# Another fixed list of steps for linear attention followed by a Fourier mix and two layers

## The chip, the core and the metric

The kernel runs on one core of one Trainium2 chip. The metric is the time of one execution on the device in microseconds (us); a run gives one such time, and the median of the runs is what is compared. A core has a matmul engine (PE, with its weight loads shown apart as PEld), a vector engine (DVE), a scalar engine (ACT), GpSimd (POOL) and a queue that mostly issues transfers (SP). Each takes its instructions strictly in the order in which they were written into its program, and they wait for one another through semaphores.

## What is computed

There are four batches with eight heads each, a sequence of 768 and a head width of 48. The first half is a linear attention with a decaying state, the second half mixes its output `x` of 768 x 384 by a Fourier transform over both axes, normalises, and adds two layers. The reference, cut to what matters:

```python
f = 1.0 / (1.0 + np.exp(-f_logit))
for t in range(S):
    state = f[:, :, t, :, None] * state + np.einsum('bhd,bhe->bhde', k[:, :, t], v[:, :, t])
    y[:, :, t] = np.einsum('bhd,bhde->bhe', q[:, :, t], state)
...
X = np.fft.fft(np.fft.fft(x, axis=1), axis=2)
u = x + np.real(X)
un = (u - mu) / np.sqrt(var + 1e-06)
out = u + np.maximum(un @ w_ch1, 0.0) @ w_ch2
```

`w_ch1` is 384 x 1536, `w_ch2` 1536 x 384. Both arrive as 64-bit floating-point words and are converted on the chip.

## The kernel before

**The list.** All the work is written as generators that do one step at a time. A string `ORDER` (lines 27 to 48) has 720 words; the loop at lines 975 to 1021 reads it word by word and runs the step that the word names, under a manual schedule. So the order of the words is the order of the instructions in the queue of each engine, and nothing is rearranged afterwards. A step writes its instructions to several queues at once, transfers on SP among them.

**Attention.** A number in the list is the next step of that unit. There are 16 units, one for two heads of one batch, four to a batch. Its steps in turn: (1) exp and ln on ACT (L372, L373); (2) the running sum of the decays on DVE (L379), and its values at the ends of chunks (L380); (3) two exp on ACT (L383, L384) and `te` (L387); (4) q and k scaled on DVE (L391, L392); (5) the scores `sc` on PE (L400); (6) masking on DVE (`copy_predicated`, L404, `at`); (7) products of masked scores with `v` on PE (L559), more scores (L576) and a copy on ACT (L579); (8) more products (L559), and the chunk states `ds` (L599); (9) their running sum on DVE (L607, `stt`); (10) the products of states and q on PE (L616) and five copies on ACT (L625 to L629); (11) transposes on PE (L636) and copies into `x` (L640, L641); (12) and, for two units of each batch, (13) the folding of `x` on DVE (L663 to L669, then L678 to L687), whose results `se`, `xs`, `ce` and `xc` are the inputs of the Fourier transform. `Kn` transposes the keys of unit n (L538, L540), `Ln` with letters loads its f, q, k (L212, L213) or v (L206, L207) on SP.

**Fourier and layers.** `Fn` is the next step of the front of batch n: four products `z` (L724) with copies on ACT, then `mid` (L758) and `mix` (L743) with sums and moments on DVE. `Hn` is the next step of what follows it: moments, normalising on DVE (`un`, L779), transposes on PE (`pt`, L782) and copies (L783). `Pn` is the next step of the two layers: for batch 0 products `up` (L871), and for its first pair of row blocks `po` (L880); for the others a scheme with fewer products that adds blocks first: `ub` (L840), with sums of inputs on DVE (L814), and sums of its results in `h` (L849) or copies (L847). The second layer is `fx` and `fz` (L894), each group followed by sums on DVE (L901 to L947) and by stores (L692, L698, L916, L931).

**Weights.** There are 24 blocks of weights. `r` issues the load of the next raw block into one of three buffers `raw` (L310), `R` three of them; `C` converts a block on ACT (L281), DVE (L283, L284) and POOL (L285). Both `fx` and `fz` need the differences of blocks that `W` makes on DVE (L358 to L361), and `ub` needs those that the words `B` make (L814, in 128 x 512). `V` and `c` read the weights once more, late, and reduce them (L344) for a check of ranges.

**The rest.** `D` is eight matmuls of a constant with itself into an unused part of a bank (L192), the spare products. `I` and `Z` set constants on POOL, `i` loads an identity, `T` and `S` load and sort the tables of the transform (S on POOL). `M` reduces the ranges met into one flag (L962 to L972, with a matmul `turned`, L969). After the list every engine loads the flag (L1023) and branches (L1025) over a rarely needed second computation.

The spare products and the loop of the list, as far as they matter:

```python
def busy():
    for _ in range(8):
        nc.tensor.matmul(spare, lhsT=bound[:, :C], rhs=bound[:, :C], start=not started, stop=True,
...
for word in ORDER.split():
...
    elif kind == "P":
        next(rest[n], None)
```

Of the kernel before, what the change touches and what calls it, by code (L numbers as in the profile page):

```python
# [12 lines left out]
C = 128  # L13
# [11 lines left out]


ORDER = (
# [20 lines left out]
)  # L48


# [1063 lines left out]
```

## Time and profile before

| | us |
|---|---|
| median of three runs | 526.31 |
| lowest and highest run | 525.15, 529.97 |
| the profiled execution, and its span | 526.26 |

In the profile a line is named by its number (L404), a product or buffer by the program's name without its number. "out<-in" gives what is written and read. Waits name the engine and the line that waited and, behind the arrow, what released it; "issue" is time in which an engine waited for nothing that the profile shows. On the timeline a row is its start, its duration, the engine, the line, the operation, the names, the shape and the number of instructions in it, and in brackets the idle time of the engine just ahead.

The execution has three stretches: the front up to the first `z` of batch 0 at 59.5 us, then the rest of batch 0 with all the weights, and from 143 us on the other three batches.

### The profile page before, as it was taken

To read this page: it belongs to the slowest core of one execution; us is meant where nothing else is said; L and a number is where in the kernel's file an instruction comes from. 1 tells how busy PE (TensorE), PEld (TensorE's weight loads), DVE (VectorE), ACT (ScalarE), POOL (GpSimd) and SP (SyncE) were. 2 spreads that over 40 slices of the span, in tenths; PEclk is the share of its full clock that TensorE was granted. 3 is DMA by queue.
4 is the path that set the end of the run, shared out by engine and by line. 5 is a ranking of instruction groups with operands and counts; after the bars stand their busy time and mean duration, and the time that the engine had idled before them with its cause. 6 is when DMAs were issued, how large, how long until landed. Compare 5 with 4: busy or idle time off the path is not lost.

```text
span 526.3 us, 13807 instructions
## 1 busy us (share of the span) xinstructions
PE 494.9 (94%) x5854; PEld 453.4 (86%) x5854; DVE 378.3 (72%) x746; ACT 218.4 (42%) x520; POOL 58.8 (11%) x85
## 2 busy tenths in 40 slices
PE   5878599999999999999999999999999999999994
PEld 4757388866899889999999999999999999999994
DVE  3598989989955368688588776779776667465571
ACT  5567368656331542453435523550431404031220
POOL 3045033551001000000001000000001000010100
PEclk9789699999999999999999999999999999999998
DMA  8957837575010230103212012120610312220200
GB/s 222 268 147 206 210 109 214 161 221 158 6 55 30 68 97 17 54 21 114 77 55 84 1 55 72 46 63 23 206 43 15 107 47 81 83 91 8 84 11 27
DMA packets 20650, 48.15 MB, mean 91 GB/s; under 512 B 3426, under 2 KB 6179, under 8 KB 20579
## 3 DMA queue, kind: packets, MB, share of 16 engines
q1 hardware_dynamic: 19474, 43.63, 29.5%
q0 software_dynamic: 1104, 3.54, 1.8%
q8 instruction: 48, 0.79, 0.6%
q14 instruction: 24, 0.19, 0.1%
HBM read 42.44 MB, written 4.72 MB: 90 GB/s over the span
## 4 chain that ended last, share of the span: by engine, by line
PE 87%; DVE 6%; issue 2%; ACT 2%; DMA 1%; POOL 0%; SPq 0%; DVEq 0%; ACTq 0%
PE ub L840 23%; PE fx L894 16%; PE fz L894 11%; PE up L871 9%; PE z L724 5%; PE y L559 4%; PE mix L743 3%; PE y L616 2%; PE sc L400 2%; PE ds L599 2%; PE po L880 2%; PE yt L636 2%; PE pt L782 1%; PE st L538 1%; PE y L192 1%
## 5 line engine op out<-in xcount | busy, mean ns | idle before, releaser
L849 DVE TENSOR_TENSOR h<-h,ub 128x512 f32<-128x512 f32 x81 | 55.2, 687 | 33.5 <-PE ub L840 24.5
L692 POOL DMA_INDIRECT out_dram<-x,place x16 | 16.4, 1024 | 357.6 <-DVE x L944 224.3
L847 ACT ACTIVATE h<-ub 128x512 f32<-128x512 f32 x54 | 31.9, 591 | 42.3 <-PE ub L840 42.3
L871 PE MATMUL up<-unT,w 128*128 128x256 f32 x216 | 49.4, 382 | 0.0
L840 PE MATMUL ub<-wide,w 128*128 128x128 f32 x360 | 45.0, 276 | 2.3 <-DVE wide L814 2.3
L894 PE MATMUL fx<-block,h 128*128 128x192 f32 x264 | 46.9, 328 | 0.0
L894 PE MATMUL fx<-w,h 128*128 128x192 f32 x264 | 45.5, 327 | 0.0
L840 PEld LDWEIGHTS ub<-wide,w 128*128 128x128 f32 x360 | 42.4, 192 | 3.4 <-PE pt L782 1.3
L871 PEld LDWEIGHTS up<-unT,w 128*128 128x128 f32 x216 | 40.1, 190 | 5.9 <-ACT h L873 0.4
L851 ACT ACTIVATE h<-h 128x512 f32<-128x512 f32 x45 | 28.4, 631 | 38.1 <-DVE h L849 37.7
L894 PEld LDWEIGHTS fx<-block,h 128*128 128x128 f32 x264 | 43.2, 190 | 0.5 <-DVE x L911 0.2
L894 PEld LDWEIGHTS fx<-w,h 128*128 128x128 f32 x264 | 42.7, 190 | 0.4 <-issue 0.2
L285 POOL TENSOR_TENSOR w<-w,raw 128x384 uint32<-128x384 uint32 x24 | 29.4, 1228 | 72.3 <-DVE w L284 39.1
L840 PE MATMUL ub<-unT,w 128*128 128x128 f32 x288 | 37.0, 275 | 0.0
L840 PEld LDWEIGHTS ub<-unT,w 128*128 128x128 f32 x288 | 34.6, 192 | 0.0
L783 ACT COPY unT<-pt 128x384 f32<-128x384 f32 x24 | 11.4, 484 | 46.8 <-PE pt L782 46.6
L840 PE MATMUL ub<-unT,wide 128*128 128x128 f32 x216 | 29.1, 278 | 0.0
L840 PE MATMUL ub<-wide 128*128 128x128 f32 x216 | 28.6, 275 | 0.1
L873 ACT ACTIVATE h<-up 128x256 f32<-128x256 f32 x36 | 13.9, 385 | 33.6 <-PE up L871 22.0
L840 PEld LDWEIGHTS ub<-unT,wide 128*128 128x128 f32 x216 | 26.4, 192 | 0.5
L840 PEld LDWEIGHTS ub<-wide 128*128 128x128 f32 x216 | 26.3, 192 | 0.3 <-PE ub L840 0.3
L379 DVE TENSOR_TENSOR_SCAN W<-g,bound 112x768 f32<-112x768 f32 x12 | 21.0, 1747 | 6.7 <-ACT g L373 6.7
(194 smaller groups left out, 1000.1 us busy)
## 6 DMA issues: line engine op xcount, KB each, us to landing
raw<-in_w_ch_dram SPq DMA_DIRECT2D x24, 384.0 KB, 5.1
v<-in_v_dram SPq DMA_DIRECT2D x16, 288.0 KB
k<-in_w_ch_dram SPq DMA_DIRECT2D x12, 384.0 KB, 3.4
g<-in_w_ch_dram SPq DMA_DIRECT2D x12, 384.0 KB, 3.3
k<-in_qkf_dram SPq DMA_DIRECT2D x14, 288.0 KB
g<-in_qkf_dram SPq DMA_DIRECT2D x12, 288.0 KB, 3.5
q<-in_qkf_dram SPq DMA_DIRECT2D x12, 288.0 KB, 3.3
wide<-in_qkf_dram SPq DMA_DIRECT2D x10, 288.0 KB, 4.7
```

Source lines behind the costliest of these rows:

```text
L285: nc.gpsimd.tensor_tensor(bits, bits, lo, ALU.add)
L379: nc.vector.tensor_tensor_scan(W, g, bound[:R], 0.0, ALU.add, ALU.min)
L559: nc.tensor.matmul(y[FILL[g], c // 3, c % 3 * C + t.start:c % 3 * C + t.stop], lhsT=vals[rows, o:o + (64 if g == 0 else D)], rhs=weights, ...
L692: nc.gpsimd.indirect_dma_start(out=out.rearrange("b s d -> (b s) d"), out_offset=bass.IndirectOffsetOnAxis(ap=place[:, b, i:i + 1], axis=0 ...
L724: nc.tensor.matmul(z[:, cols], lhsT=src[:, j, lo:hi], rhs=tab[:, t, T % 2, cols], start=(i == 0), stop=(i == len(parts) - 1), skip_group_c ...
L743: nc.tensor.matmul(mix[:, o], lhsT=zz[:rows_of[T], T, PLACES[c]], rhs=cd[:rows_of[T], T, :NQ - odd], start=(i == 0), stop=(i == 1))
L840: nc.tensor.matmul(chains[chain][:, m * 128:(m + 1) * 128], lhsT=block(w)[:, m * 128:(m + 1) * 128], rhs=tokens(a), start=(new and m == 0) ...
L847: nc.scalar.activation(out, got, kind, scale=1.0 if how == "=+" else -1.0)
L849: nc.vector.tensor_tensor(out, out, got, ALU.add if how == "+" else ALU.subtract)
L851: nc.scalar.activation(out, out, AF.Relu)
L871: nc.tensor.matmul(pp[:, :256], lhsT=w1[:, kt, m * 128:(m + 1) * 128], rhs=unT[:, kt], start=(kt == 0), stop=(kt == 2))
L894: nc.tensor.matmul(out, lhsT=h[:, m], rhs=blocks[i][:, m], start=(start and m == 0), stop=(m == H - 1), skip_group_check=True)
```

## The change

Only the string `ORDER` differs. It holds the same words, each as many times as before, in another sequence, so every engine gets the same work in another order (and a few instructions that only wait come out otherwise). The diff, cut to the three places that matter here, the start, the way to the first `F0`, and the end:

```diff
-    "L0f Z I 0 L0q L2q D D L1f L0k D 0 D 0 i D 1 L2f 2 0 D D D L0v 0 L1k K0 D 0 0 D L1q 0 1 D r 1 L3fk D "
-    "D D L1v 2 0 L2k 1 D r r D 1 2 1 3 3 0 C K1 1 2 0 C 1 L3q 2 1 3 C L2v 2 r K2 L4fk 3 L3v L5fk 1 2 1 D "
-    "T 2 0 4 3 D C S 1 2 5 3 D 2 3 2 4 K3 3 D L5qv L4qv 5 4 3 2 3 L6fk 3 2 3 5 R 3 F0 F0 4 6 F0 L6qv F0 C "
...
-    "V P3 P3 c P3 V P3 c P3 c P3 P3 V c c P3 P3 P3 P3 P3 P3 M P3 P3 P3 P3 P3 P3 P3 P3"
+    "I L0f 0 0 i L1f 1 0 L0k L0q Z L2f 2 L0v 0 0 L1q 1 1 D L1k 0 K0 0 2 1 L3fk L2q 3 L1v D D 0 L2k 0 2 1 "
+    "1 r 0 L3q K1 L2v D 1 3 2 0 C 1 1 2 2 3 1 D D r 1 L5fk L4fk L3v T 3 2 r K2 L4qv 5 C L6fk 1 3 2 3 4 D "
+    "D 2 5 2 D 3 0 2 K3 4 3 3 D 3 D 2 2 D 3 D 3 L5qv 4 3 5 4 D D D r D D D 5 L7fk S F0 F0 F0 F0 4 C 4 C 6 "
+    "K4 F0 R D D 4 5 7 4 C H0 H0 4 4 5 K5 L6qv H0 C 5 C r 6 r P0 P0 r 5 C 7 6 6 C P0 P0 5 P0 6 C r 6 7 C "
...
+    "P3 P3 P3 P3 P3 P3 P3 P3 P3 P3 P3 P3 P3 P3 P3 P3 P3 P3 P3 P3 P3 P3 P3 V P3 P3 c P3 P3 M"
```

Three places in the queues follow, first as they stood and then as they stand. In a row stands the line, the operation, the names with the numbers of their buffers and the shape.

The vector engine near the start, where units 0 and 1 (`at_91` and `at_92`) are under way; before:

```order
L404 COPY_PREDICATED at_91<-causal,sc_0_237 128x768
L379 SCALAR_TENSOR_TENSOR W_352<-g_86,bound 112x768
L380 TENSOR_TENSOR deep<-g_86,W_352 112x6
L379 SCALAR_TENSOR_TENSOR W_400<-wide,bound 112x768
L380 TENSOR_TENSOR deep<-wide,W_400 112x6
L607 SCALAR_TENSOR_TENSOR stt_403<-ds_341,te_98 112x288
L391 TENSOR_TENSOR q_90<-q_90,g_86 112x768
L392 TENSOR_TENSOR g_86<-W_352,k_88 112x768
L404 COPY_PREDICATED at_92<-causal,sc_0_429 128x768
```

And now:

```order
L379 SCALAR_TENSOR_TENSOR W_198<-g_86,bound 112x768
L380 TENSOR_TENSOR deep<-g_86,W_198 112x6
L404 COPY_PREDICATED at_91<-causal,sc_0_171 128x768
L379 SCALAR_TENSOR_TENSOR W_249<-wide,bound 112x768
L380 TENSOR_TENSOR deep<-wide,W_249 112x6
L391 TENSOR_TENSOR q_90<-q_90,g_86 112x768
L392 TENSOR_TENSOR g_86<-W_198,k_88 112x768
L607 SCALAR_TENSOR_TENSOR stt_319<-ds_306,te_98 112x288
L404 COPY_PREDICATED at_92<-causal,sc_0_324 128x768
```

The scan of unit 1 (`W` of `g_86`) now stands ahead of unit 0's masking, and unit 1's two scalings ahead of the running sum of unit 0's states (L607).

The matmul engine at unit 1's scores (`sc_0_429` before, `sc_0_324` after); before, the last of 48 spare products ahead of them and what follows:

```order
L192 LDWEIGHTS bound
L192 MATMUL y<-bound 128x128
L400 MATMUL sc_0_429<-q_90,g_86 64x64 x24
L616 MATMUL y<-q_89,stt_403 48x128 x10
L538 MATMUL st_483<-ident,g_86 128x112 x5
```

And now:

```order
L599 MATMUL ds_306<-v_165,kT_221 64x48x2
L599 MATMUL ds_306<-v_165,kT_221 48x48x2
L400 MATMUL sc_0_324<-q_90,g_86 64x64 x24
L616 MATMUL y<-q_89,stt_319 48x128 x10
L538 MATMUL st_370<-ident,g_86 128x112 x5
L192 LDWEIGHTS bound
L192 MATMUL y<-bound 128x128
```

The scores of unit 1 now follow unit 0's states at once, and the spare products come behind the transposed keys.

The vector engine at the end of the list; before, with eight steps of `P3` still to come:

```order
L849 TENSOR_TENSOR h_3_2_5090<-h_3_2_5090,ub_2_1_5092 128x4x128
L962 TENSOR_REDUCE part<-deep 112x1
L963 TENSOR_REDUCE part<-hot 112x1
L964 TENSOR_REDUCE most<-small 128x1
L965 TENSOR_SCALAR most<-most 128x1
L966 SCALAR_TENSOR_TENSOR most<-part,most 112x1
L967 SCALAR_TENSOR_TENSOR most<-part,most 112x1
L970 TENSOR_REDUCE most<-turned 1x1
L972 TENSOR_SCALAR flag<-most 1x1
L901 TENSOR_TENSOR s_3_2_5214<-h_3_2_5090 128x768
```

And now:

```order
L344 TENSOR_REDUCE small<-g_85 128x1
L927 TENSOR_TENSOR x_3907<-fx_2_5192,x_3907 128x384
L930 TENSOR_TENSOR x_3907<-fz_2_5210,x_3907 128x192
L962 TENSOR_REDUCE part<-deep 112x1
L963 TENSOR_REDUCE part<-hot 112x1
L964 TENSOR_REDUCE most<-small 128x1
L965 TENSOR_SCALAR most<-most 128x1
L966 SCALAR_TENSOR_TENSOR most<-part,most 112x1
L967 SCALAR_TENSOR_TENSOR most<-part,most 112x1
L970 TENSOR_REDUCE most<-turned 1x1
L972 TENSOR_SCALAR flag<-most 1x1
L1023 TENSOR_LOAD flag
```

The flag is now made behind the last sum of the second layer, and the load of the flag follows it.

32 rows, old and new, of the table ORDER are left out of this document.

## The prediction, made before the changed kernel ran

> **What bounds the kernel now.** I read the page first, then windows by stage, then the waits of DVE and PE at the front, then their timelines. The profiled execution lasted 526.26 us, 0.05 us off the median of the three runs, so the sum needs no correction.
>
> The windows view gives busy time by engine, the granted clock (PEclk) and the DMA share for a stretch:
>
> ```profile
> core 0: us, PE busy (x) PEld busy (x) DVE busy (x) ACT busy (x) POOL busy (x), PEclk, DMA share, GB/s
> 0.00:59.50 59.50, 39.77 (x940) 34.57 (x940) 41.90 (x69) 36.78 (x77) 18.15 (x49) 0.85 0.84 220
> 17.70:24.50 6.80, 6.17 (x69) 5.83 (x70) 2.57 (x3) 3.68 (x6) 0.00 (x0) 0.50 1.04 284
> 55.20:65.50 10.30, 5.96 (x14) 3.89 (x15) 9.65 (x23) 3.77 (x12) 0.00 (x0) 0.50 0.75 205
> 59.50:143.30 83.80, 82.27 (x1084) 64.58 (x1085) 76.48 (x128) 50.46 (x128) 25.73 (x21) 0.96 0.52 146
> 143.30:519.40 376.10, 372.81 (x3832) 354.25 (x3830) 259.55 (x550) 131.18 (x315) 14.87 (x15) 1.00 0.20 60
> ```
>
> From 143.3 to 519.4 us PE is busy in 372.81 of 376.10 us. The edit adds no matmul but moves some, so at most 3.3 us is to be had there. From 59.5 to 143.3 PE has 1.5 us of idle time, DVE 7.3. Only the front, up to the first z product of batch 0, leaves 19.7 us of PE idle, and part of the PE time is spare products. PE starts z when DVE has made `se` (last row but one of the next fence), so the front is DVE's: 41.9 us of work in 59.5. The first stage that can shrink is that one. Its DVE waits, then its PE rows, its DVE rows, and the packets around a PE gap:
>
> ```profile
> DVE W L379 <- ACT g L373: 6.5, 1, 6.5
> DVE at L404 <- PE sc L400: 4.3, 2, 3.1
> DVE stt L607 <- PE ds L599: 4.2, 2, 2.8
> DVE q L391 <- ACT g L383: 1.0, 1, 1.0
> ...
> 4.60 5.08 PE L192 MATMUL y<-bound 128*128 128x128 bf16 x64 [4.60 <-POOL bound L175]
> 18.33 0.48 PE L559 MATMUL y<-at,v 64*48 64x64 f32 x7 [2.25 <-issue]
> 20.11 4.93 PE L192 MATMUL y<-bound 128*128 128x128 bf16 x48
> ...
> 20.23 0.76 DVE L607 TENSOR_TENSOR_SCAN stt<-ds,te 112x288 f32<-112x288 f32 x1 [2.82 <-PE ds L599]
> 21.92 0.96 DVE L392 TENSOR_TENSOR g<-W,k 112x768 f32<-112x768 f32 x1
> 25.96 1.04 DVE L404 COPY_PREDICATED at<-causal,sc 128x768 f32<-128x768 uint32 x1 [3.08 <-PE sc L400]
> ...
> q1 hardware_dynamic: 177, 0.43, 100.7%
> q8 instruction: 1, 0.02, 5.0%
> ...
> 58.98 0.46 DVE L681 TENSOR_TENSOR se<-xs 128x285 f32<-128x285 f32 x1
> 59.54 2.85 PE L724 MATMUL z<-tab,se 128*95 128x385 f32 x6 [4.38 <-issue]
> ```
>
> The reader is to see two chains in it. Unit 1's inputs of its scores are complete at 22.88 (L392, 21.92 + 0.96), yet 48 spare products stand ahead of those scores in PE's queue, from 20.11 to 25.04, at granted clock 0.50. DVE then waits 3.08 us in L404. Before that, L607 waits 2.82 us for `ds`, because PE stood still 2.25 us ahead of 18.33 with nothing to wait for. In those microseconds (15.5 to 17.0) the input loads (q1) fill the DMA engines to 100.7% of their time, and one packet of instructions (q8) is among them. I read that gap as a late piece of PE's program.
>
> [...]
>
> **The front, costed.** The changed list puts unit 1's scan (L379) ahead of unit 0's L404, so DVE has work while it waits; it issues no spare products at all ahead of unit 0's scores and none between unit 0's `ds` and unit 1's scores; two blocks of weights fewer are converted before z; and the spare products (7 words, 56 matmuls) now stand right ahead of z, where PE waits for DVE anyway. Up to `se` the changed DVE queue holds 64 instructions instead of 68: the four of two conversions less (0.9 us each, rows further down), so 41.9 - 1.8 = 40.1 us of work. The 59.44 us of before are 41.9 of work, 16.0 in these four waits and 1.5 of gaps. The first wait, 6.5 us for exp and ln, stays, and so does the 1.0 of L391. Of the 8.5 us in L404 and L607 I keep 4: 2 for unit 0's scores and states, whose chain is serial, and 2 for the units behind, since a walk by hand along the changed queues with these durations finds DVE waiting for PE only up to unit 2. 40.1 + 1.5 + 6.5 + 1.0 + 4 = 53.1; I take z to begin at 53.0, against 59.54: -6.5 us. Bounds: with only the first two waits left, 49.1 (-10.4); with all of L404's and L607's waits but the 3.08 of the spare products, and one more stall of 2.25, 56.8 (-2.7).
>
> Removing the first 64 spare products costs nothing by itself: PE has nothing else to do before unit 0's scores.
>
> [...]
>
> **z itself.** In 55.2 to 65.5 the clock is 0.50, so z's first 6 us (from 59.54) ran at half rate. With 56 spare products just ahead they should run at full rate, some 3 us less of PE. I count 0 for it, because DVE decides what follows:
>
> **From z to the first `fz`.** `fz` (L894) needs `block` from L361.
>
> ```profile
> 141.88 1.36 DVE L361 TENSOR_TENSOR block<-w,block 128x1152 f32<-128x1152 f32 x1
> 154.32 1.95 PE L894 MATMUL fz<-block,h 128*128 128x192 f32 x11
> ...
> 58.49 0.46 DVE L678 TENSOR_TENSOR xs<-eo 128x288 f32<-128x288 f32 x1
> 61.12 0.56 DVE L687 TENSOR_TENSOR xc<-xc 128x384 f32<-128x384 f32 x1
> 133.24 0.45 DVE L663 TENSOR_TENSOR eo<-x 128x288 f32<-128x288 f32 x1
> 135.41 0.34 DVE L669 TENSOR_TENSOR eo<-x 1x192 f32<-1x192 f32 x1
> L779 DVE TENSOR_SCALAR un<-x,mv,rstd 128x384 f32<-128x384 f32 x24 | 11.1, 470 | 0.8 <-ACT rstd L770 0.5 <-PE pt L782 0.3
> L814 DVE TENSOR_TENSOR wide<-wide,w 128x512 f32<-128x512 f32 x5 | 3.4, 683 | 0.0
> ```
>
> Before, DVE ends L361 at 143.24, 83.8 us after `se` (59.44), while PE needs 94.8 us from z to `fz` (154.32 - 59.54): DVE is 11.1 us ahead. PE's set of products between the two is the same, but for 8 more spare ones (0.4 us or so). DVE's is not: 151 instructions instead of 127. It gains two folds (L663 to L669, 2.5 us each by the rows at 133.24 and 135.41), one set of sums and differences (L678 to L687, 3.2 by the rows at 58.49 and 61.12), two conversions (next fence, 0.9 each), one L404 (1.0), one L607 (0.8), two L779 (0.9), and loses five weight sums (L814, 0.68 each, 3.4): 5.0 + 3.2 + 1.8 + 1.0 + 0.8 + 0.9 - 3.4 = +9.3. So DVE would end 93.1 us after `se`, with its lead nearly gone.
>
> The weights come through three raw buffers:
>
> ```profile
> 73.93 0.33 DVE L283 TENSOR_SCALAR w<-raw 128x384 uint32<-128x384 uint32 x1
> 74.29 0.56 DVE L284 SCALAR_TENSOR_TENSOR w<-raw,w 128x384 uint32<-128x384 uint32 x1
> 117.00 0.56 DVE L284 SCALAR_TENSOR_TENSOR w<-raw,w 128x384 uint32<-128x384 uint32 x1
> L285 POOL TENSOR_TENSOR w<-w,raw 128x384 uint32<-128x384 uint32 x24 | 29.4, 1228 | 72.3 <-DVE w L284 39.1 <-ACT raw L281 29.0 <-DVE un L779 3.7
> L281 ACT ACTIVATE raw<-raw,two 128x384 f32<-128x384 uint32 x24 | 15.6, 665 | 2.9 <-DMA raw<-in_w_ch_dram 2.7
> SPq L310 <- POOL w L285: 41.8, 16, 11.4
> DMA to landing us min/median/max: 3.1/5.1/5.5
> ```
>
> Before, blocks 8 to 24 took 42.7 us of DVE's time (74.29 to 117.00), 2.67 each, where the instructions themselves sum to 2.36 each. After, blocks 3 to 24 stand in one run (21 steps of 2.35 by the same means), the three fetches of `R` come behind the load L7fk, whose buffer comes free only with unit 4, so after z. At the same 2.67 the five steps more cost 5 x 0.31 = 1.6, so DVE ends at 94.7: level with PE's 94.8. Two chains that are level, and that hand work to each other, end later than either; I add 1.5 for that and the spare products. Bounds: -2.5 (PE alone, z at full rate, 0.5 for spare products) and +6 (a ring at 2.9).
>
> **Batches 1 to 3.** The same 3832 products less the tail; DVE has 259.55 of 376.10 us there, so re-mixing them leaves the 3.3 us of PE idle about as it is: 0, between -1 and +3 (all of it again). The loads of later units hide behind 0.20 DMA share.
>
> **The tail.** The check of ranges (M) moves from ahead of the last eight steps to the very end:
>
> ```profile
> 504.08 0.24 DVE L962 TENSOR_REDUCE part<-deep 112x1 f32<-112x96 f32 x1
> 505.21 0.38 PE L969 MATMUL turned<-ident,most 128*1 128x128 f32 x2 [0.73 <-DVE most L967]
> 505.94 0.14 DVE L972 TENSOR_SCALAR flag<-most 1x1 int32<-1x1 f32 x1
> 519.86 0.36 SPq L931 DMA_DIRECT2D out_dram<-x  x1
> SPq L1025 <- SPq L1025: 2.5, 1, 2.5
> ```
>
> It saves PE the wait and the two matmuls in the middle, 0.73 + 0.38 less an overlap, 1.0 us. It puts L962 to L972, 2.0 us (504.08 to 506.08), behind the last DVE step, 0.4 of it beside the issue of the last store on SP (519.86): +1.6. Then the branch follows, 2.5 us, as before. Net +0.6; bounds -1 (the engines' loads of the flag were late anyway) and +2.
>
> **Sum.** 526.3 - 6.5 + 0 + 1.5 + 0 + 0.6 = 521.9; I say 522.
>
> **The rivals.**
> - *All of it arrives.* PE, not DVE, leads to `fz` and z runs at full rate: 526.3 - 6.5 - 2.5 + 0.6 = 517.9, down to 515 if z begins at 50 too. For it: DVE is only just level by the count. Against: it must be level at every hand-over.
> - *The raw buffers' ring eats it, or more than it* (the slower side). Each block's way is 5.1 us of landing and 0.33 + 0.56 + 0.67 + 1.23 = 2.8 of conversion; with one L404 (1.04) in between, (5.1 + 2.8 + 1.04) / 3 = 2.98 us per block, 21 x 0.31 = +6.5 beyond 94.7 and thus 526.3 - 6.5 + 6.5 + 0.6 = 526.9. With 5.5 for each landing and two such copies it is 3.5 and 537. The point at which it decides is 2.95 per block. For it: SP waits 41.8 us for these buffers already. Against: before's own pace was 2.67.
> - *The start is slow in the new order.* Half rate or a late piece of the program keeps z at 56.8: 526.3 - 2.7 + 1.5 + 0.6 = 525.7, or with nothing gained at the front 528.4. For it: half rate and the 2.25 us stand in the rows above. Against: PE isn't the bound of that stage.
>
> **How the numbers follow.** Forecast (519 to 525) 0.5; all of it (515 to 519) 0.2; ring or slow start up to 531.6, 0.23; ring beyond that, 0.07. The range leaves out a little on each side: 516 to 530.5. A measurement of this kernel tells about 1% from no change: faster than 521.0 is the second case and a good third of the first, 0.39; slower than 531.6 is 0.07; the rest is 0.54.
>
> **What would show it.** Front: z at 53 in the changed profile, no L404 wait over 2 us, no 48 spare products at 20. If z is later than 57, my front is wrong. Middle: L361 ending some 94 us after `se`, `fz` about 96 us after z, SP's waits for L285 more than 41.8 in total. If `fz` comes 92 us after z, the first rival holds; at 100 or more, the ring's. Tail: the last product of PE about 1 us nearer to `ub`, and some 2 us between the last store's issue and the branch. If the stretch from `fz` to the end changes by over 2 us in any direction, the zero for batches 1 to 3 is wrong.

## The result and the profile after

| | before | after |
|---|---|---|
| median of nine runs, us | 527.71 (523.83 to 529.97) | 535.26 (531.72 to 537.31) |
| ratio, with its 95% interval | | 1.013 (1.0094 to 1.0165) |
| span of the profiled execution, us | 526.26 | 533.07 |

The changed kernel is 1.3% slower. The forecast was 522, with 516 to 530.5 as its range: the wrong side. The spans differ by 6.8 us, so the profiles show nearly all of it. (In the nine runs of the changed kernel the time lies 1.7 to 2.2 us above the span: the profiled run of the changed kernel took 535.26 us with a span of 533.1. The forecast took the span of before for its time and so stood about 1.8 us too low for this alone.) One profile, that of the kernel without the spare products between a unit's steps, was taken in an execution 1.6% longer than the fastest of that kernel, so its stretches are weak evidence below.

Four stretches cut both executions at the same work: the front up to the first product of the first `z`, the middle up to the first `fz`, the batches up to the last group of 24 `fx` products, and the end. The windows view of the kernel before, then of the changed one; the columns are those of the forecast's first fence:

```profile
0.00:59.54 59.54, 39.77 (x940) 34.60 (x941) 41.94 (x69) 36.78 (x77) 18.15 (x49) 0.85 0.84 220
59.54:154.32 94.78, 93.29 (x1296) 74.77 (x1296) 83.39 (x141) 55.47 (x139) 25.73 (x21) 0.97 0.48 136
154.32:505.52 351.20, 347.91 (x3537) 330.42 (x3536) 246.47 (x524) 126.17 (x304) 14.87 (x15) 1.00 0.20 62
505.52:526.26 20.74, 13.91 (x85) 13.62 (x84) 6.50 (x13) 0.00 (x0) 0.00 (x0) 0.92 0.08 25
```

```profile
0.00:57.70 57.70, 37.07 (x932) 32.77 (x933) 39.69 (x65) 35.43 (x75) 16.33 (x47) 0.94 0.84 213
57.70:153.79 96.09, 92.99 (x1303) 73.56 (x1304) 89.05 (x154) 56.60 (x142) 28.20 (x23) 1.00 0.51 143
153.79:509.75 355.96, 350.82 (x3535) 332.68 (x3534) 244.10 (x508) 125.38 (x303) 14.61 (x15) 1.00 0.20 60
509.75:533.05 23.30, 14.20 (x88) 13.64 (x86) 7.85 (x20) 0.99 (x2) 0.00 (x0) 0.90 0.13 39
```

The second number of a row is its length. The front lost 1.84 us (forecast: 6.5), the middle grew by 1.31 (forecast: 1.5), the batches by 4.76 (forecast: -1.0, for the flag's pause, which goes to the end) and the end by 2.56 (forecast: 1.6). The loss thus lies behind the first `fz`, where I had looked least.

The waits of DVE up to z in the changed kernel, and two of PE's waits in the whole execution:

```profile
DVE W L379 <- ACT g L373: 6.5, 1, 6.5
DVE eo L663 <- ACT x L641: 3.5, 2, 2.5
DVE at L404 <- PE sc L400: 2.6, 1, 2.6
DVE stt L607 <- PE ds L599: 2.5, 3, 1.1
DVE q L391 <- DMA q<-in_qkf_dram: 1.3, 1, 1.3
...
PE y L559 <- DVE at L404: 2.2, 1, 2.2
PE sc L400 <- issue: 2.1, 1, 2.1
```

DVE has less work in the front than before (39.69 us instead of 41.94), but behind the first wait it still waits 9.9 us, where before it was 9.7 (L404, L607, L391 and L663). The waits only sit elsewhere. Two of PE's rows matter below: 2.1 us of "issue" in unit 1's scores, and 2.2 us for a masking (L404) deep in the batches.

### The profile page after: what moved, and what is told of

Read it like the earlier page. It is cut to its first block, busy times and chain, and to the rows that moved or that the text cites. A ratio compares the mean times of both kernels' runs of the same rounds, so it can differ in the third digit from the quotient of the medians.

```text
span 533.1 us, 13821 instructions
## 1 busy us (share of the span) xinstructions
PE 495.1 (93%) x5854; PEld 452.6 (85%) x5854; DVE 380.7 (71%) x746; ACT 218.4 (41%) x520; POOL 59.1 (11%) x85
## 4 chain that ended last, share of the span: by engine, by line
PE 70%; DVE 5%; DMA 5%; ACT 1%; issue 1%; POOL 1%; SPq 0%; ACTq 0%; POOLq 0%
PE ub L840 23%; PE fx L894 15%; PE fz L894 12%; PE up L871 6%; PE z L724 3%; PE mix L743 2%; DMA g<-in_qkf_dram 2%; PE y L559 2%; DMA raw<-in_w_ch_dram 2%; PE pt L782 1%; PE sc L400 1%; PE y L616 1%; PE ds L599 1%; PE yt L636 1%; DVE w L284 1%
## 5 line engine op out<-in xcount | busy, mean ns | idle before, releaser
L871 PE MATMUL up<-unT,w 128*128 128x256 f32 x216 | 50.6, 385 | 0.2 <-DVE x L884 0.2
L894 PE MATMUL fx<-block,h 128*128 128x192 f32 x264 | 46.6, 327 | 0.0
L894 PE MATMUL fx<-w,h 128*128 128x192 f32 x264 | 45.9, 328 | 0.0
L894 PEld LDWEIGHTS fx<-block,h 128*128 128x128 f32 x264 | 43.3, 190 | 0.1
L894 PEld LDWEIGHTS fx<-w,h 128*128 128x128 f32 x264 | 42.7, 190 | 0.4
L400 PE MATMUL sc<-q,g 48*64 48x64 f32 x576 | 12.1, 229 | 13.9 <-DVE g L392 11.8
```

The lines of the kernel that those rows point to most:

```text
L400: nc.tensor.matmul(own[64 * s:64 * s + 64, r, c * 64:c * 64 + 64], lhsT=g[ROWS[r], o:o + 64], rhs=Q[ROWS[r], o:o + 64], start=True, stop=True)
L871: nc.tensor.matmul(pp[:, :256], lhsT=w1[:, kt, m * 128:(m + 1) * 128], rhs=unT[:, kt], start=(kt == 0), stop=(kt == 2))
L894: nc.tensor.matmul(out, lhsT=h[:, m], rhs=blocks[i][:, m], start=(start and m == 0), stop=(m == H - 1), skip_group_check=True)
```

## The experiments

All stretches below are cut as above and are of one profile each; total times are medians of all runs, and ratios are to the kernel before in the same series. The diffs show only the words around an edit.

**The end: the check early again.**

```diff
-... P3 V P3 P3 c P3 P3 M
+... V P3 P3 P3 P3 P3 P3 P3 P3 P3 P3 c M P3 P3 P3 P3 P3 P3 P3 P3
```

> The changed list with the check of ranges (M) ahead of the last eight steps again, and the last reload (V) and its reduction (c), which M needs, ahead of it. Theory: the changed kernel loses at its end because all engines load the flag and take the branch together, only after the last sum; with M early, the end (from the first of the last 24 fx to the end) falls from 23.30 to 20.7 us, the wait of SP at the branch from 3.9 to 2.5 us, and PE loses about 1.0 for the flag's matmuls again: some 531.4 in all against 533.05. Rival: the end is longer for another reason (clearing after more transfers in flight), so it stays at 23 and the kernel gets 1 us slower, 534.

Its end took 20.53 us (23.30 in the changed kernel), and SP waits 2.5 us at the branch as in the kernel before. The batches took 356.38, 0.4 more. The time didn't show it, 535.12 us, 1.0135 (1.0081 to 1.0189), since z began 1.3 us later and the middle took 1.2 more in this profile. The mechanism held, the total of 531.4 did not come.

**The end: the check last in the list of before.**

```diff
-... V c c P3 P3 P3 P3 P3 P3 M P3 P3 P3 P3 P3 P3 P3 P3
+... V c c P3 P3 P3 P3 P3 P3 P3 P3 P3 P3 P3 P3 P3 P3 M
```

> The list of before with the check of ranges (M) as its last word and nothing else changed. Theory (all engines load the flag and branch together, after the last sum): the end grows from 20.74 to 23.4 us, the wait of SP at the branch from 2.5 to 3.9 us, and PE has about 1.0 us less ahead of the last eight steps; the kernel is some 1.6 us slower than before (1.003). My prediction's reading (the branch stays at 2.5 us): 0.6 us slower, the end 22.3.

Measured: 1.0035 (1.0001 to 1.0069), the end 24.35 us (3.6 more than before, where 2.7 was expected), the batches 349.88. SP's waits here (its lines stand one lower):

```profile
SPq L1026 <- SPq L1026: 3.8, 1, 3.8
SPq L1024 <- DVE flag L973: 1.5, 1, 1.5
```

SP waits for the flag for 1.5 us, which the forecast had (1.6), and 3.8 at the branch, which it hadn't: it took over 2.5. In the trace of the kernel before, ACT and POOL load the flag and branch at 506 us and PE at 517, in the shadow of the last products; PE's branch alone takes 3.6 us. With the check last, all five do it in the same microsecond (525.91 to 526.8 in the changed kernel), and there the branches take 3.2 to 3.9 us. SP's ends last, with 3.9 instead of 2.5. In that kernel the only packets that the DMA engines move from 526.4 to 530.5 us are six packets of instructions. Whether the branches wait for these was not tried, and why a branch takes longer when all five engines branch at once stays open.

**The batches: one swap.** In the timeline of the changed kernel, PE stands still for unit 15's masking; the first rows are PE's, the others DVE's:

```profile
349.27 2.22 PE L894 MATMUL fx<-w,h 128*128 128x192 f32 x12
353.72 0.57 PE L559 MATMUL y<-at,v 64*48 64x64 f32 x24 [2.23 <-DVE at L404]
354.57 0.90 PE L782 MATMUL pt<-ident,un 128*128 128x128 f32 x3
...
351.52 0.36 DVE L905 TENSOR_TENSOR x<-fx,x 128x192 f32<-128x192 f32 x1 [2.53 <-PE fx L894]
352.66 1.00 DVE L404 COPY_PREDICATED at<-causal,sc 128x768 f32<-128x768 uint32 x1
```

DVE waits 2.53 us in L905 for `fx`, and L404, whose scores were done at 349.3, stands behind it. PE waits for L404, and after the pause its products run at half rate: the granted clock is 0.50 from 354.5 to 357.9 us, and three `pt` take 0.90 us where they take 0.49 at 346.04.

```diff
-K15 H2 P2 V c 15 P2 15 15 H2 13 12 12
+K15 H2 P2 V c 15 15 P2 15 H2 13 12 12
```

> The changed list with one swap: the masking step of unit 15 (L404) stands ahead of the step of the second layer whose sum L905 waits for fx. Theory: the 2.23 us in which PE waits for L404 and the half clock behind it (some 1.9) are this order's alone; the stretch from the first fz to the last fx group falls from 355.96 to about 352, the total from 533.05 to 529. Rival: PE meets another wait right behind (the folds), and the stretch falls by less than 1 us.

The same place after the swap:

```profile
349.08 2.22 PE L894 MATMUL fx<-w,h 128*128 128x192 f32 x12
351.22 0.57 PE L559 MATMUL y<-at,v 64*48 64x64 f32 x24
353.09 0.52 PE L782 MATMUL pt<-ident,un 128*128 128x128 f32 x3 [0.95 <-DVE un L779]
```

The wait is gone, and the batches took 352.81 us, 3.15 less; the time was 532.67, 1.0113 (1.0069 to 1.0157). This interval overlaps that of the changed kernel, so the evidence here is the stretch. PE now comes to `pt` earlier than `un`, which stands behind the two sums L905 and L906 as before, and waits 0.95 us for it.

**Both edits.**

> The changed list with both edits that worked alone, the check of ranges ahead of the last eight steps and unit 15's masking ahead of the sum that waits for fx. If they add up, the stretch from the first fz to the last fx group is 353 to 354 (the flag's pause back in it), the end 20.7, and the kernel some 5.5 us faster than the changed one: 529.5, which is 1.004 to 1.006 of before. If they don't (one wait hides the other), 531 or more.

530.6 us, 1.0069 (1.0041 to 1.0096): batches 354.96, end 20.62. They add up to somewhat less than forecast, and half of the loss is gone.

**Both edits, and `un` three words later.**

```diff
-K15 H2 P2 V c 15 15 P2 15 H2 13 12 12
+K15 H2 P2 V c 15 15 P2 15 13 12 12 H2
```

> The changed list with the check early, unit 15's masking ahead of the sum, and the step that normalises and transposes (H2) behind it three words later. If the 0.95 us in which PE waits for un (L779) in the run with both edits is a plain wait, it goes, and the stretch from the first fz to the last fx group falls from 355.0 to 354. If the folds that now stand ahead of un only move it, the stretch stays at 355 or grows.

The wait did not go, it grew:

```profile
PE pt L782 <- DVE un L779: 5.1, 1, 5.1
```

Two folds of seven instructions (L663 to L669) now stand ahead of `un` on DVE; the batches took 361.13 us and the kernel 536.65, 1.0213 (1.0157 to 1.027). One word moved by three places was worth 6 us (361.13 against 354.96).

**Later words as before.** The changed list up to the first F1, then what is left in the order of before (the check early with it); at the seam:

```diff
-P0 P0 P0 P0 P0 F1 P0 K8 F1 F1 F1 8 8 L10fk ...
+P0 P0 P0 P0 P0 B B B B B P0 P0 P0 P0 P0 B P0 ...
```

> The changed list up to the first step of batch 1's front (F1), then the words that are left in the order of before, the check of ranges ahead of the last eight steps with them. Theory (up to the first fz the two orders are worth the same, within the scatter of z; the later batches and the end carry the loss): 154 to 156 us to the first fz, 351 to 352 to the last fx group, 20.7 for the end, and a time within 0.4% of before. Rival (the changed front or middle leaves the loss behind for the batches): 354 or more there, and the kernel still 1% slower.

525.72 us, 0.9991 (0.9956 to 1.0026): no difference from before. Its batches took 351.02 us, its end 20.51 and its middle 96.09, as in the changed kernel. So the changed front and middle hand nothing on; the later words carry the loss.

**The front alone.** The changed list up to the fourth F0, then what is left in the order of before:

```diff
-5 L7fk S F0 F0 F0 F0 4 C 4 C 6 K4 F0 R D D 4 5 ...
+5 L7fk S F0 F0 F0 F0 C C D R 6 L6qv C C 4 C 4 F0 ...
```

> The changed list up to the fourth F0, then the words that are left in the order of before. Theory (the changed front is worth 2 us, the full rate of z 2.9, and the later order and the end lose it): z at 55.5 plus 0 to 4 us for stalls of PE's program, 92 to 93 us to fz, then 351.2 and 20.7 as before: 520 to 524. Rival (the front itself brings the loss, by what it leaves behind for later, for instance loads of weights that come too late): the stretch from z to fz is 95 or more, and the kernel no faster than before.

1.0124 (1.0076 to 1.0173). z began at 58.88, batches 351.88 and end 20.79, but 100.47 us for the middle. By its signs the rival's case came, and loads that came too late were the cause: PE waits 6.8 us at one place (`st`, L538) for a masking behind conversions whose blocks had not landed. But that place is the seam, where neither of the two orders stands as it was written, so the run says nothing of the changed front in its own list; there the middle took 96.09.

**The 48 spare products ahead of unit 1's scores** (left out).

```diff
-0 1 D r 1 L3fk D D D L1v 2 0 L2k 1 D r r D 1
+0 1 r 1 L3fk L1v 2 0 L2k 1 r r 1
```

> The list of before without the six words of spare products (48 matmuls, left out) ahead of unit 1's scores. My prediction's reading: they cost the 3.08 us in which L404 waits, so L404 waits under 0.5 there and z begins about 2.5 us earlier than 59.54 (57), the kernel about 523.5 where before is 526. Rival: the copies, states and folds of the next units set the pace (one unit's products wait for the copies of the one before), so the wait turns up again in L607 or L663, z begins at 59 to 60 and the time is as before.

The rival was right. L404 did come 3.4 us earlier (22.53 instead of 25.96), but z began at 59.51 and the kernel took 1.0058 (1.0036 to 1.0079). L607 waits 6.4 us in all, where it was 4.2. The same six words put right ahead of z instead:

```diff
-R 3 F0 F0 4 6 F0
+R 3 D D D D D D F0 F0 4 6 F0
```

> The list of before with those six words moved to right ahead of z, so nothing is left out. Theory: z runs at full rate (5.4 us from its first product to the next scores instead of 8.3) and, as PE and not DVE sets the pace from z to the first fz, that stretch falls from 94.8 to 92 us; with z 0 to 2.5 us earlier the kernel is 3 to 5 us faster than before (0.99). My prediction's reading (DVE is level with PE there): with before's DVE 11 us ahead the gain shows here as well, so only a stretch of 94 to 95 us would speak against both.

z ran at full rate (5.37 us for its four groups, at a granted clock of 0.97 from 60 to 68 us; 7.3 to 8.3 in the three profiles of before), but it began at 62.49, so the products behind it began at 67.86 us, 67.84 before. The middle took 93.87, where the theory had 92; three profiles of the kernel before's own middle took 93.6 to 97.2. 1.0016 (0.9991 to 1.0041): nothing.

**The 2 us in which PE stands still.** I counted PE's records (weight loads and its waits on semaphores too) up to each gap of more than 0.8 us in the front that the waits view calls "issue" and that lies inside a unit's products or the spare ones:

```
kernel                    instruction number: us
before                    449: 2.25
before, once more         449: 1.56   705: 1.26
before, check last        449: 2.17
changed                   449: 2.09
check early               449: 0.83   705: 0.96   1217: 2.96
one swap                  449: 2.02   1217: 1.86
both edits                449: 1.99   1217: 2.61
both, un later            449: 1.33
front alone               449: 2.85   1217: 2.44
z at half rate            449: 1.87   1217: 1.83
loads ahead               449: 1.59   1217: 1.59
24 spare products less    705: 3.17
64 spare products more    705: 1.84   1473: 1.42
later words as before     1217: 1.04
48 spare products less    449: 1.34   705: 0.96
those 48 ahead of z       449: 2.38   705: 0.82
none between steps        449: 1.37   1217: 2.53
```

The numbers are 449 plus a multiple of 256, in kernels whose 449th instruction is another one. Two of these kernels were made for that:

```diff
-0 0 i L1f ... 1 1 D L1k ... L1v D D 0
+0 0 i L1f ... 1 1 L1k ... L1v 0
```

> The changed list without the first three words of spare products (24 matmuls, 48 instructions of PE, left out). In both traces PE stands still for 2 us at its 449th instruction, in another line each time. Theory: the gap goes with the number of the instruction, so it now stands in unit 0's last products (L616) and not in unit 1's scores; the wait of L404 for them falls from 2.56 to under 0.6, and z begins 1 to 2 us earlier. Rival: it goes with the time (20 us, when the loads fill the DMA engines): it stays in the scores at 19 to 22 us, the wait stays above 2 and z at 57 to 58.

No gap at 449; one of 3.17 us at 705, in products of L559 and not in L616; z at 58.65, and 1.0136 (1.01 to 1.0172). So the gap goes with the number, but which of the numbers shows it changes from run to run.

```diff
-I L0f 0 0 i
+I L0f 0 D D D D D D D D 0 i
```

> The changed list with eight more words of spare products (64 matmuls, 128 instructions of PE) at the start, in time in which PE waits for the first inputs, as before had them. If half rate in the first units is what holds the front back, unit 0's scores take 1.0 instead of 1.7 us, and z begins 1 to 2 us earlier than in the runs of the same front (57.7, 59.0, 58.1). If the chain over DVE, ACT and the one result buffer does, z stays at 57 to 59. The stalls of PE's program should stand at the instruction numbers 449, 705, 961 and 1217 again, so in other lines than in the changed kernel (449 now in unit 0's products, L559).

z began at 57.51, inside the scatter of the same front without them; 1.0155 (1.0127 to 1.0183). But the edit did not do what it was made for:

```profile
11.26 1.66 PE L401 MATMUL sc<-q,g 48*64 48x64 f32 x48 [3.21 <-DVE g L393]
```

PE was through with the spare products at 8.05 us and stood still for 3.21 us ahead of unit 0's scores (the lines stand one lower), which took 1.66 us, as long as in the changed kernel; in the kernel before they take 1.03. So it stays open what the slower products in the first units cost. The gaps stood at 705 and 1473.

**Spare products between a unit's steps** (five words left out).

```diff
-3 1 D D r 1 ... 4 D D 2 5 2 D 3 0 2 K3 4 3 3 D 3 D 2 2 D 3 D 3
+3 1 r 1 ... 4 D D 2 5 2 3 0 2 K3 4 3 3 D 3 2 2 3 D 3
```

> The changed list without the five words of spare products (40 matmuls, left out) that stand between a unit's last products and its transposes or next products in the front. Theory: they stand on the way from the copies of yT over the transposes and the copies to x to the folds; the 2.54 and 1.0 us in which L663 waits for L641 shrink by some 1.6 and 0.8, and z begins at about 55.3 instead of 57.70. Rival: without them the clock is at half rate for longer and nothing is gained: z between 57 and 58.

1.0126 (1.0071 to 1.018): nothing is gained, as the rival had it. In its profile L663 waits 0.8 us instead of 3.5, but L607 9.7 instead of 2.5, and z began at 59.59: by this profile the wait moved on.

**The middle: z at half rate, and the loads of weights.**

```diff
-3 D 3 L5qv 4 3 5 4 D D D r D D D 5 L7fk S F0
+3 3 L5qv 4 3 5 4 r 5 L7fk S F0
```

> The changed list without the seven words of spare products (56 matmuls, left out) ahead of z. Theory (from z to fz PE sets the pace, not DVE): z runs at half rate, its four groups take 8.3 instead of 5.4 us, and the stretch from z to the first fz grows by all of it, from 96.1 to about 99. My prediction's reading (DVE decides there): the stretch stays at 96 to 97. In both, z begins at about the same time (57.5 to 59.5, by the stalls of PE's program).

1.0166 (1.0127 to 1.0205). z's four groups took 8.0 us (the first two 2.85 and 2.76, where in the kernel before they take 2.85 and 2.77 at a granted clock of 0.50) and the middle 97.94. Eight profiles with this middle and full rate took 95.8 to 97.3, 96.5 in the mean, so of 2.6 us more, some 1.4 arrived. That is one profile, 0.6 us above the longest of the eight. It lies between the two expectations and settles neither.

```diff
-D D D r D D D 5 L7fk S F0 F0 F0 F0 4 C 4 C 6 K4 F0 R D D
+D D D r D D D 5 R L7fk S F0 F0 F0 F0 4 C 4 C 6 K4 F0 D D
```

> The changed list with the three loads of raw weights (R) ahead of the load L7fk, behind which they wait for unit 4. My prediction's rival (the three buffers set the pace from z to fz): the stretch from z to the first fz falls by 1 us or more below 96.1, the waits of L283 for the loads (1.3) vanish. Theory (PE sets it, the buffers don't matter): it stays within 1 us of 96, the waits of L283 fall but PE's own waits and products do not.

538.38 us, 1.021 (1.0181 to 1.0239), the middle 102.96. SP, ACT and PE in turn:

```profile
SPq L310 <- POOL w L285: 20.2, 3, 14.9
...
ACT wide L372 <- DMA wide<-in_qkf_dram: 5.1, 1, 5.1
...
PE pt L782 <- DVE un L779: 4.7, 1, 4.7
```

SP stood at the third load until its buffer was free, and the loads of units 7 and 6 behind it went out late (the first at 66.70 us). ACT waited 5.1 us for one of them with the copies that everyone needs queued behind, and PE got `un` 4.7 us late. The order that I had listed as a danger (R behind L7fk) was the better one.

**The front of before, once more.**

> The kernel before, once more with its profile, as a third start of the same front: the two so far began z at 59.54 and 57.98 us, and five profiles of the changed front at 57.7 to 59.0. If the changed front has a gain of 2 us or more, z begins here at 60 or later; if the fronts are worth the same, between 57.5 and 59.6.

z began at 58.01, with 525.47 us in all. By this expectation the two fronts are worth the same.

## Why the prediction was wrong

**The front: -6.5 forecast, -1.84 in the profile.** The step that failed here is the one that kept 4 of the 8.5 us of waits in L404 and L607, let the others go and put no wait in their place. In the changed kernel these two wait 5.1 us, and L663 waits 3.5 us for ACT's copies (L641), a term that the sum did not have: the waits moved from the scores to the copies. With 0.3 more in L391 and 0.4 less of work this makes up the 4.6 us between 53.1 and 57.7. Profiles of before's front (the kernel with the check last has it too) began z at 57.98, 58.01 and 59.54, 58.5 in the mean. Those of the changed front: 53.60, 54.31, 56.30, 57.70, 58.11, 58.22, 58.46, 58.88 and 59.02, 57.2 in the mean (in 56.30 and 58.46 an edit stands just ahead of z). That is a gain of about 1.3 us in a scatter of 5.
- The reading of the 3.08 us as the price of 48 spare products was wrong. Taken away, they gave nothing at z; what they held up was not the last thing to arrive.
- The 2.25 us ahead of L559 came again, as 2.09 us in unit 1's scores, and L404 waited 2.56 us for it. They belong to a number in PE's program, not to the work that stood there. I had it only in the upper bound, once; profiles show one to three of them.
- 53.0 was not a bad figure for a front without them: the two starts with the least (1.04 and 1.33 us) began z at 54.31 and 53.60, the two with 2.09 and 3.17 us at 57.70 and 56.30, the five with 3.7 to 5.3 us at 58.1 to 59.0. That the gaps alone make the scatter is argued from these figures, and not shown.

**z at full rate: 0 forecast.** z took 5.38 us at a granted clock of 1.00 instead of 8.30 at 0.64 in the mean, as the step said, and the stretch to `fz` wasn't shorter. The reason given, that DVE decides, is neither borne out nor refuted: with z at half rate again the middle was some 1.4 of 2.6 us longer, in one profile.

**The middle: +1.5 forecast, +1.31 measured.** The two rows in the changed kernel:

```profile
150.34 1.36 DVE L361 TENSOR_TENSOR block<-w,block 128x1152 f32<-128x1152 f32 x1
153.79 2.11 PE L894 MATMUL fz<-block,h 128*128 128x192 f32 x12
```

DVE ended L361 at 151.70, 94.1 us after `se` (57.60), where 94.7 was forecast. PE came to `fz` 2.1 us later still, without a pause there, so DVE's lead was small but not gone. The sum held, the cause only in part: PE is idle for 3.1 us in the middle instead of 1.5, in seven small waits for DVE and ACT. Three profiles with before's middle took 93.60, 94.78 and 97.15, so 1.3 is within scatter, and that the number came out so closely is luck in part. The rival of the three buffers is not borne out: SP waits 38.0 us for them in this middle, and 41.8 before. Putting their loads ahead did not test it by itself, since SP then held up two units' loads.

**The batches: 0 forecast for the new mixing (-1.0 with the flag's pause), +4.76 measured.** This is the step that failed and that decides the result. It was an argument from sums: DVE is busy for 259.55 of 376.10 us, so its slack would cover any new mixing. Slack in a sum does not help an instruction that stands behind a waiting one. One pair of words cost 3.15 us, and the later words of before brought the whole stretch back to 351.02. The 2.6 us beyond the swap (352.81 against 351.20, less 1.0 for the pause that before has there) are the wait for `un`, 0.95, and a pace of PE's products that differs by line: in sum 0.6 us more in L616, 0.4 in L894, 0.3 in L743 and 0.2 in L782, against 0.3 less in L538 and 0.2 less in L599. What makes this pace differ stays open.

**The end: mis-sized.** The flag's way was right (1.5 us), the branch was taken as a constant of 2.5. It takes SP 3.6 to 4.1 in the eight profiles in which all five engines branch at once, and 2.5 to 2.7 in the nine in which ACT, POOL and PE branch earlier. By itself the late check costs 1.0035 in the list of before.

The front was out by 4.7 us, the batches by 5.8, the end by 1.0 and the middle by -0.2: 11.2 us of span. The slower case that I had named (the buffers of raw weights) was not the one that came. Two of the signs that I had given for a wrong step did come: z later than 57, and the stretch from `fz` to the end changed by over 2 us.

None of the kernels beats the one before beyond its interval; the one with the later words as before is level with it.

## What to carry to other kernels

When a list of steps is shuffled, the free time of an engine in a stretch says nothing about a given place: for each waiting instruction look at what is queued behind it, and who waits for that, in the late, crowded stages as well. A wait seen in one profile is worth its length only if what it holds up is the last to arrive; leave the suspect out and look at the stage's end. A pause with no cause shown may belong to the instruction's number in its engine's program (here 449 and multiples of 256 more), so it is not won by moving the work.

## What the runs showed of the hardware

PE's pauses of more than 0.8 us in the front stood at its instructions 449, 705, 1217 and 1473, that is 449 and multiples of 256 more. They lasted 0.8 to 3.2 us, and each of the 17 profiles has one to three of them. In the kernel before and in the changed one, one packet of instructions was on its way just ahead of the pause at 449 (within 15.5 to 16.0 us and within 19.0 to 19.5), while loads took all of the DMA engines' time (106.6% and 105.7% by the packets' own times).

Further on such pauses are rare but not absent: 1.00 and 1.02 us at instruction 2497 (the kernels with no spare products between steps and with 64 more, at 77.6 and 70.9 us), and 1.21 and 0.91 us at 3265 and 8129 in the kernel with 48 spare products less (at 104.0 and 310.6 us). These numbers, too, are 449 and multiples of 256 more.

That PE waits there for a piece of its program is my reading of this spacing and of the two packets; no run shows it. That the loads delay the packet was not tried by itself.
